# Where the values of a unit and the decay sums of the next stand among TensorE's products, and which queue issues the seam

## The chip, the cores and the metric

The kernel runs on one core of one Trainium2 chip. The metric is the device time of one execution in microseconds (us). Each execution is one launch, and the kernel before was run three times.

The engines are named as in the profile: PE is TensorE (matmul), PEld its weight load, DVE is VectorE, ACT is ScalarE, POOL is GpSimd, SP is SyncE. Each of them takes its instructions in the order of its own queue. POOL, ACT and SP also issue DMAs, and an issue stands in the queue like any other instruction.

## The reference

The first half is a gated recurrence over a sequence. For batch b (4), head h (8) and time t (768), with head size D = 48:

```python
mag = np.sqrt(a_re * a_re + a_im * a_im)
scale = np.minimum(mag, 0.999) / (mag + 1e-06)
a_re_n, a_im_n = (a_re * scale, a_im * scale)
for t in range(S):
    new_re = ar * S_re - ai * S_im      # ar, ai: a_re_n, a_im_n at time t
    new_im = ar * S_im + ai * S_re
    kv = np.einsum('bhd,bhe->bhde', k[:, :, t], v[:, :, t])
    S_re, S_im = (new_re + kv, new_im)
    y[:, :, t] = np.einsum('bhd,bhde->bhe', q[:, :, t], S_re)
```

The second half is a dense block on the result, laid out as 3072 tokens of 384 numbers: `h = x @ w_in` (384 by 2048), an ELU (`h` where it is positive, else `exp(h) - 1`), and `g @ w_out` (2048 by 384).

## The kernel before

**Units.** The work is cut into NU = 12 units. A unit is a chunk of C = 128 time steps of NB = 2 sequences, that is 256 tokens. Units 0 and 1 are the first chunks of the two pairs of sequences, units 2 and 3 the second chunks, and so on, so unit u + 2 carries on the state of unit u.

**The gates of a unit.** The recurrence is computed in chunks of L = 64 steps. The logarithm of the magnitudes and the angles of the gates are summed along time with matmuls, and q and k are scaled by the exponentials and turned by the sines and cosines of these sums. For a unit u > 1 the steps are: `squares` (ACT, L709 and L710), `joined` (the sum of the squares; POOL from unit 3 on, L716), `logarithms` (ACT, L735 and L736), `lengths` (DVE, L772), `powers` (ACT, L746 and L747), `ratios` (POOL, L759 and L760), `slopes` (DVE, L780), `angles` (ACT arctangent, L815), `carried` (DVE, L821, adds the angle of the chunk before to the first row), `turns` (PE sums at L832, DVE L837 and L840), `waves` (ACT sines, L967 to L971). `quartered` is the sum of the logarithms: four matmuls on PE (L883). `quarters_used` turns it into the factors E and F by six activations on ACT (L898), and writes the rows at the chunk's ends to a buffer in DRAM (L902), from where POOL fetches them as T (L951).

**The attention part of a unit.** `transposed` (PE L1013, ACT L1014) lays q and k with heads in the columns. From unit PAIRED = 4 on, `scored` is the first group of small products: the state products of both halves (L1054), then the scores of both (L1125), which DVE masks (L1133); the states are added on DVE (L1069) and scaled on POOL (L1071). `valued` is the second group: values times scores (L1087) and state times queries (L1096), both into the PSUM tile y; ACT copies y into the SBUF tiles x and y (L1156 and L1157). The heads do not fill x evenly, so `seam` moves six blocks of 16 partitions from y into x by DMA (L1169).

**The dense part of a unit.** `inner` multiplies x by w_in (L1189), `elu` applies the activation (ACT L1198 and L1199, DVE L1200). The second matmul is done by a scheme of seven products over four blocks: `folded` forms sums of blocks of g (DVE L1273), and `product(u, k, h)` does product k for half h, four matmuls each (L1295). They run in the order k = 1, 4 (half 0), 1, 4 (half 1), then 6, 5, 7, 2, 3, and gather in three PSUM banks. Product 1 is copied aside by ACT once its half 1 is done (L1303), and product 6 goes into the same bank and waits for that copy. DVE and ACT add up the rest (L1307, L1316, L1320, L1314), and SP sends the output (L1317). The matmuls are in fp32; the trace shows each as two pieces, so `x16` in it is eight matmuls of the program.

**The order.** Nothing is scheduled by a tool: the program writes the instructions in the order of a plan. The first part is a list by hand. For the rest, `put(at, fn, ...)` gives each step a due time, and the steps are written out by due time. A unit has SLOTS = 16 due times, and unit u starts at r = 16 (u - 2). Units overlap: while unit u is in its dense part, unit u + 1 is in its attention part and unit u + 2 in its gates. So due time r + 31 of unit u is r + 15 of unit u + 1.

In the kernel before, `valued` of units 4 to 10 stands at r + 31 and does three things: the values of both halves, then `quartered(u + 1)`, then the products with the state; after them it calls `quarters_used(u + 1, ...)`, and only then come the copies of y. `gates_of` therefore leaves out `decays` (which would call the same two functions) for units above PAIRED. The last unit, 11, has nobody after it, and its `valued` stands at r + 29.3. `seam` is issued from SP for the units from 4 on, from POOL for units 2 and 3.

Of the kernel before, what the change touches and what calls it, by code (L numbers as in the profile page):

```python
# [505 lines left out]
def kernel(  # L506
# [15 lines left out]
    NI, NF = DM // C, DF // C  # L522
# [3 lines left out]
    NU = B // NB * (S // C)  # L526
# [44 lines left out]
    def work(shape, tag="w"):  # L571
        return ps.tile(shape, FP32, tag=tag, bufs=3, name=tag)


    nat = [{} for _ in range(NU)]
# [110 lines left out]
    def flat(t):  # L686
        return t.rearrange("p n h d -> p (n h d)")
# [5 lines left out]
    def new(tag, bufs=1, shape=None):  # L693
        return sb.tile(shape or [C, NB, H, D], FP32, tag=tag, bufs=bufs, name=tag)
# [182 lines left out]
    def quartered(u):  # L877

        x = nat[u]
        both = [work([C, HD]) for n in range(NB)]  # L880
        for c in range(C // L):
            for n, t in enumerate(both):
                nc.tensor.matmul(  # L883
                    t[ts(c ^ n, L)], lhsT=sum_logs[ts(c, L), ts(c, L)],
                    rhs=flat(x["l"][ts(c, L), n : n + 1]), start=True, stop=True,
                )
        return both

    def quarters_used(u, both):

        x = nat[u]
        for n, t in enumerate(both):
            for key, sign in (("E", 1.0), ("F", -1.0)):
                pairs = [(slice(0, C), slice(0, C))]
                if n:
                    pairs = [(ts(c, L), ts(1 - c, L)) for c in range(C // L)]
                for to, of in pairs:
                    nc.scalar.activation(  # L898
                        out=flat(x[key][to, n : n + 1]), in_=t[of], func=AF.Exp, scale=sign
                    )  # L900
        ends = dram.tile([NB, C // L, H, D], FP32, tag="ends", bufs=2, name="ends")
        nc.scalar.dma_start(  # L902
            out=ends.rearrange("n c h d -> c n (h d)"),
            in_=x["E"][L - 1 :: L].rearrange("p n h d -> p n (h d)"),
        )
        x["ends"] = ends

    def decayed(u, n):
        x = nat[u]
        t = x["sums", n]  # L910
        for key, sign in (("E", 1.0), ("F", -1.0)):
            if u > 0 and n == 0:
                x[key] = new("n", 6)
            nc.scalar.activation(
                out=flat(x[key][:, n : n + 1]), in_=t, func=AF.Exp, scale=sign
            )

    def decays(u):
        x = nat[u]
        if u > 1:  # L920
            x["E"], x["F"] = new("n", 6), new("n", 6)
            quarters_used(u, quartered(u))
            return
        for n in range(NB):
            x["sums", n] = work([C, HD])
            nc.tensor.matmul(
                x["sums", n], lhsT=sum_logs, rhs=x["l"][:, n].rearrange("p h d -> p (h d)"),
                start=True, stop=True,
            )
            decayed(u, n)  # L930
# [68 lines left out]
    PAIRED = 4  # L999
# [83 lines left out]
    def value_products(u, n, y, first=True):  # L1083
        x = nat[u]
        for p, c, j in EACH:

            nc.tensor.matmul(  # L1087
                y[ts(j, HP), c, ts(p, L)], lhsT=vn[u % 2][ts(c, L), n, ds((2 * p + j) * D, HP)],
                rhs=x["a", n][ts(c, L), 2 * p + j], start=(first and p == 0), stop=False,
                skip_group_check=True,  # L1090
            )
    def carried_products(u, n, y):
        x = nat[u]
        for p, c, j in EACH:
            if x["S", n][c] is not None:
                nc.tensor.matmul(  # L1096
                    y[ds(j * HP, D), c, ts(p, L)], lhsT=x["S", n][c][:, 2 * p + j],
                    rhs=x["qt", n][:, 2 * p + j, ts(c, L)], start=False, stop=False,
                    skip_group_check=True,
                )  # L1100
# [37 lines left out]
    def valued(u):  # L1138

        x = nat[u]  # L1140
        y = ps.tile([C, C // L, 512], FP32, tag="y", bufs=1, name="y")
        for n in range(NB):
            value_products(u, n, y[:, :, ts(n, NP * L)], n == 0)
        if u + 1 < NU:
            both = quartered(u + 1)
        for n in range(NB):
            carried_products(u, n, y[:, :, ts(n, NP * L)])
        if u + 1 < NU:
            z = nat[u + 1]
            z["E"], z["F"] = new("n", 6), new("n", 6)  # L1150
            quarters_used(u + 1, both)
        x["x"], x["y"] = new("x", 2, [C, NI, GT]), new("y", 1, [C, GT])
        parts = y.rearrange("p c (n x t) -> p c n x t", n=NB, x=NP)
        to = x["x"].rearrange("p x (n c t) -> p c n x t", n=NB, c=C // L)
        for c in range(C // L):
            nc.scalar.copy(out=to[:, c], in_=parts[:, c, :, 0:NI])  # L1156
        nc.scalar.copy(  # L1157
            out=x["y"].rearrange("p (n c t) -> p c n t", n=NB, c=C // L), in_=parts[:, :, :, NI],
        )

    def seam(u):

        x = nat[u]
        for j in range(2):
            for i in range(NI):
                eng = nc.scalar if u < 2 and j else nc.gpsimd
                if u >= PAIRED or u == 0 and i == NI - 1:
                    eng = nc.sync
                eng.dma_start(  # L1169
                    out=x["x"][ds(j * HP + D, G), i], in_=x["y"][ds(j * HP + i * G, G)]  # L1170
                )
# [232 lines left out]
    def put(at, fn, *args):  # L1404
        if fn is hidden:
            plan.append((at, len(plan), inner, args))
            plan.append((at, len(plan), elu, args))
        else:
            plan.append((at, len(plan), fn, args))

    def decays_of(u, *at):
        fns = squares, logarithms, powers, lengths, ratios, slopes, noted, angles, carried
        put(at[0], begun, u)
        for x, fn in zip(at, fns):
            put(x, fn, u)
            if fn is squares:
                put(x, joined, u)

    def gates_of(u, *at):
        for x, fn in zip(at, (decays, turns, waves, scaled, ends, gated)):  # L1420
            if fn is not decays or u <= PAIRED:
                put(x, fn, u)

    def values_of(u, *at):
        fns = (transposed, "q"), (transposed, "k"), (scores,), (states,), (values,)
        for n in range(NB):
            for x, (fn, *key) in zip(at[5 * n :], fns):
                put(x, fn, u, *key, n)
        put(at[-1], seam, u)
# [64 lines left out]
    def layer_of(u, at_h, at_p):  # L1494
        for m in range(NF // 2):
            put(at_h[m], hidden, u, 2 * m)
        put(at_h[3], folded, u, 0)
        put(at_h[7], folded, u, 1)
        ks = [(1, 0), (4, 0), (1, 1), (4, 1)] + [(k, h) for k in (6, 5, 7, 2, 3) for h in range(2)]
        for m, (k, h) in enumerate(ks):  # L1500
            put(at_p[0] + m * len(at_p) / len(ks), product, u, k, h)

    for u in range(2, NU):
        r = (u - 2) * SLOTS
        put(r + 8, load_a, u)
        put(r + 8, load_v, u)
        put(r + 8, load_qk, u)
        if u == 2:
            decays_of(u, 16, 17, 17, 18.4, 19.5, 19.6, 22.7, 19.8, 19.8)
            gates_of(u, 20.4, 21.6, 22.1, 22.4, 22.4, 22.6)  # L1510
        else:
            decays_of(u, r + 11, r + 12, r + 12, r + 13.4, r + 13.5, r + 14.9, r + 16.7, r + 15.5, r + 16.6)
            gates_of(u, r + 15, r + 18, r + 18.5, r + 18, r + 18, r + 19.5)
        if u < PAIRED:
            values_of(u, *(max(r + 22, 24.5) + x for x in (0, 1, 2, 3, 5, 4, 5, 6, 7, 8, 9)))
        else:
            for n in range(NB):
                put(r + 22 + 2 * n, transposed, u, "q", n)
                put(r + 23 + 2.3 * n, transposed, u, "k", n)
            put(r + 26.6, scored, u)  # L1520
            put(r + (31 if u + 1 < NU else 29.3), valued, u)
            put(r + (31 if u + 1 < NU else 29.3), seam, u)
        layer_of(u, range(r + 36, r + 44), range(r + 44, r + 52))
    for m in range(NR):
        put(40 + 4 * m, test_fetch, m)
# [42 lines left out]
```

## Time and profile before

| | |
|---|---|
| three runs | 730.99, 731.03, 733.4 us; median 731.03 |
| the profiled execution | 733.4 us, span 731.7 us from first to last instruction |
| PE busy | 677.1 us, 93% of the span, 6656 instructions |
| PEld busy | 593.2 us, 81% |
| ACT busy | 398.5 us, 54% |
| DVE busy | 395.9 us, 54% |
| POOL busy | 176.0 us, 24% |
| mean granted clock of PE | 0.966 of full speed |
| HBM | 48.88 MB read, 4.78 MB written, 73 GB/s over the span |

How to read the lines that follow. A line of the timeline gives the start and the length in us, the engine, the line of the program, the operation, output and inputs by the program's names, partitions and shape, and how many such instructions in a row. Brackets at its end give the idle time ahead of it and who ended it. A length covers the time from the first start to the last end, and matmuls overlap a little, so from one group's start to the next group's start is the better measure of what a group takes. A line of the table of stages gives the window, its length, the busy time of PE, PEld, DVE, ACT and POOL with instruction counts, then the granted clock of PE, the share of the DMA engines and GB/s. A line of the view of waits names the waiting instruction, the one that released it, the total in us, how often, and the longest.

In this kernel the steady part, units 4 to 10, repeats with a period of 57.7 to 59.4 us; the seven stretches look alike, and the one from 430 to 462 us stands for them below.

### The profile page before, as it was taken

The page shows a single profiled execution, that of the slowest core. Times are in us where ns is not written, and L with a number is a line of the kernel's source. Part 1 is how long each engine was busy: PE and PEld are TensorE (multiplying, and loading weights), DVE is VectorE, ACT ScalarE, POOL GpSimd, SP SyncE. Part 2 cuts the span into 40 slices and gives each one's busy share as a digit, 9 for nine tenths or more (in the row PEclk, how much of TensorE's full clock was granted, in tenths as well). Part 3 has the DMA queues.
Part 4 walks back from the last instruction along what each step waited for, and adds up shares of the span by engine and source line. Part 5 has one row for each costly group of instructions (what it writes and reads, how often), then busy time and mean ns, then how long its engine had stood idle before and what let it go on. Part 6 is the DMA issues. An engine that isn't in the chain of part 4 may idle for free.

```text
span 731.7 us, 15769 instructions
## 1 busy us (share of the span) xinstructions
PE 677.1 (93%) x6656; PEld 593.2 (81%) x6656; DVE 395.9 (54%) x579; ACT 398.5 (54%) x622; POOL 176.0 (24%) x159
## 2 busy tenths in 40 slices
PE   8798899988999979979979998997997997999996
PEld 6787775665889879879879887997987986989995
DVE  5789999516666545454454553553644545433141
ACT  6765446578466456645653754655546654661230
POOL 2000000237145133151331431422413403310000
PEclk9889999999999989989999999998999999999999
DMA  9986555232536403701901901920730550200000
GB/s 166 168 144 110 141 172 130 51 61 50 77 77 110 93 23 88 115 22 49 154 23 40 142 23 33 152 41 25 125 77 22 116 86 24 72 1 7 22 1 27
DMA packets 149899, 55.98 MB, mean 77 GB/s; under 512 B 129172, under 2 KB 142652, under 8 KB 149820
## 3 DMA queue, kind: packets, MB, share of 16 engines
q1 hardware_dynamic: 147776, 54.32, 39.1%
q0 software_dynamic: 1824, 0.44, 0.8%
q8 instruction: 54, 0.88, 0.5%
q14 instruction: 25, 0.20, 0.1%
q10 hardware_dynamic: 220, 0.14, 0.1%
HBM read 48.88 MB, written 4.78 MB: 73 GB/s over the span
## 4 chain that ended last, share of the span: by engine, by line
PE 73%; issue 6%; ACT 5%; DVE 5%; POOL 5%; SPq 3%; DMA 2%; ACTq 0%; POOLq 0%; DVEq 0%
PE mlp L1189 28%; PE mlp L1295 22%; PE w L1013 5%; PE mlp L1210 4%; PE y L1096 3%; PE w L1054 2%; POOL n L716 2%; SPq L596 2%; PE y L1125 2%; PE y L1087 2%; PE w L832 2%; POOL S L1071 1%; PE w L1210 1%; ACT n L746 1%; ACT n L736 1%
## 5 line engine op out<-in xcount | busy, mean ns | idle before, releaser
L1189 PE MATMUL mlp<-x,w_in 128*128 128x256 f32 x1152 | 260.6, 381 | 2.6 <-DVE g L1200 2.6
L1189 PEld LDWEIGHTS mlp<-x,w_in 128*128 128x128 f32 x1152 | 214.6, 190 | 31.9 <-DVE g L1200 3.0
L1198 ACT ACTIVATE ee<-mlp 128x512 f32<-128x512 f32 x96 | 57.3, 597 | 144.1 <-PE mlp L1189 135.8
L1200 DVE SCALAR_TENSOR_TENSOR g<-ee,mlp 128x512 f32<-128x512 f32 x96 | 65.5, 685 | 126.2 <-ACT ee L1199 116.6
L1295 PE MATMUL mlp<-w_out,g 128*128 128x192 f32 x640 | 110.3, 326 | 0.0
L1295 PEld LDWEIGHTS mlp<-w_out,g 128*128 128x128 f32 x640 | 105.4, 190 | 2.7
L1295 PE MATMUL mlp<-w,g 128*128 128x192 f32 x320 | 70.5, 384 | 28.4 <-ACT ee L1303 28.4
L1295 PEld LDWEIGHTS mlp<-w,g 128*128 128x128 f32 x320 | 64.3, 227 | 31.9 <-ACT ee L1303 30.5
L1071 POOL TENSOR_TENSOR S<-S,T 128x384 f32<-128x384 f32 x36 | 29.3, 830 | 168.4 <-DVE S L1069 168.4
L1273 DVE TENSOR_TENSOR g<-g 128x512 f32<-128x512 f32 x80 | 67.2, 841 | 2.7
L1199 ACT ACTIVATE ee<-ee 128x512 f32<-128x512 f32 x96 | 60.5, 631 | 2.9
L898 ACT ACTIVATE n<-w 64x384 f32<-64x384 f32 (+1 forms) x60 | 28.1, 486 | 49.3 <-PE w L883 48.6
L856 POOL DMA_DIRECT2D carry<-n x10 | 5.3, 530 | 172.9 <-DVE n L840 172.9
L993 POOL TENSOR_TENSOR kg<-k,cs 128x1536 f32<-128x1536 f32 x9 | 41.0, 4551 | 20.1 <-issue 20.0
L1314 ACT COPY o<-mlp 128x192 f32<-128x192 f32 x10 | 3.2, 319 | 67.1 <-DMA out_dram<-o 56.3
L821 DVE SCALAR_TENSOR_TENSOR n<-carry,n 1x768 f32<-1x768 f32 x10 | 9.5, 946 | 45.3 <-ACT n L815 45.3
L1210 PE MATMUL mlp<-w_out,g 128*128 128x384 f32 x96 | 32.8, 490 | 0.7 <-DVE g L1200 0.7
L1014 ACT COPY qt<-w 128x512 f32<-128x512 f32 x48 | 25.6, 581 | 12.5 <-PE w L1013 12.5
L1295 PE MATMUL mlp<-wt,g 128*128 128x192 f32 x160 | 29.2, 327 | 0.0
L993 DVE TENSOR_TENSOR qg<-q,cs 128x1536 f32<-128x1536 f32 (+1 forms) x12 | 19.5, 1623 | 17.4 <-ACT cs L971 17.4
L716 POOL TENSOR_TENSOR n<-n 128x768 f32<-128x768 f32 x9 | 19.8, 2196 | 35.4 <-ACT n L710 35.4
L1013 PE MATMUL w<-ident,kg 128*128 128x128 f32 x192 | 26.0, 280 | 2.3 <-POOL kg L993 1.4
(173 smaller groups left out, 981.4 us busy)
## 6 DMA issues: line engine op xcount, KB each, us to landing
w<-in_moe_w_out_dram SPq DMA_DIRECT2D x8, 768.0 KB, 4.9
g<-in_moe_w_in_dram SPq DMA_DIRECT2D x16, 384.0 KB, 3.2
g<-in_moe_w_out_dram SPq DMA_DIRECT2D x16, 384.0 KB, 3.4
w<-in_moe_w_in_dram SPq DMA_DIRECT2D x16, 288.0 KB, 5.9
vn<-in_v_dram SPq DMA_DIRECT2D x24, 192.0 KB, 4.0
out_dram<-o SPq DMA_DIRECT2D x48, 96.0 KB, 2.1
ar<-in_a_re_dram SPq DMA_DIRECT2D x22, 192.0 KB, 4.6
ai<-in_a_im_dram SPq DMA_DIRECT2D x22, 192.0 KB, 7.5
```

The source lines that it names most:

```text
L716: products(u).tensor_tensor(out=x["m2"], in0=x["m2"], in1=x["sq"], op=ALU.add)
L898: nc.scalar.activation(out=flat(x[key][to, n : n + 1]), in_=t[of], func=AF.Exp, scale=sign)
L993: eng.tensor_tensor(out=to[:, :, :, 0:D], in0=each.unsqueeze(2).to_broadcast([C, step * H, 2, D]), in1=x["cs"][:, n * H : (n + step) * H], ...
L1013: nc.tensor.transpose(t[:, h], of, ident)
L1071: eng.tensor_tensor(out=new_s, in0=new_s, in1=wide, op=ALU.mult)
L1189: nc.tensor.matmul(t[:, e], lhsT=w_in[:, i, ts(f + e, C)], rhs=x["x"][:, i], start=(i == 0), stop=(i == NI - 1),)
L1198: nc.scalar.activation(out=e, in_=t, func=AF.Relu, scale=-1.0)
L1199: nc.scalar.activation(out=e, in_=e, func=AF.Exp, scale=-1.0)
L1200: nc.vector.scalar_tensor_tensor(out=x["g", f // 8][:, f % 8 : f % 8 + 2], in0=e, scalar=-1.0, in1=t, op0=ALU.add, op1=ALU.max)
L1210: nc.tensor.matmul(x["o", n], lhsT=x["g", f // 8][:, f % 8, ts(n, C)], rhs=w_out[:, f], start=(f == 0), stop=(f == NF - 1),)
L1273: nc.vector.tensor_tensor(out=S_of(u, k, h), in0=a, in1=b, op=op)
L1295: nc.tensor.matmul(to, lhsT=a[:, m], rhs=b[:, m], start=(first and h == 0 and m == 0), stop=False, skip_group_check=True,)
```

## The change

- `quartered` and `quarters_used` become one function again, `quartered`, which does the four sums, the six activations and the DMA of the ends. It is called by `decays`.
- `decays` is put for every unit, at its own due time r + 15. That is the place in the queues of PE and ACT where the four sums stood before; what is new is that they stand there alone.
- `valued` and `seam` stand at r + 29.3 for every unit, so for units 4 to 10 they move ahead by 1.7 due times. The products of L1295 that lie between are passed by `valued` on PE: k = 4 half 1 and both halves of k = 6. On ACT the copies of y now stand behind L1303 and ahead of the six activations of the next unit.
- `seam` of units 4 to 11 is issued by POOL. In POOL's queue the six DMAs of unit u (4 to 10) stand behind L716 and ahead of L759 and L760 of unit u + 1. They leave SP's queue, where they stood between two fetches of weights.

The order of the first group of small products is not touched, and the order of DVE's instructions is the same in both programs.

```diff
--- before.py
+++ after.py
@@ -884,11 +884,6 @@
                     t[ts(c ^ n, L)], lhsT=sum_logs[ts(c, L), ts(c, L)],
                     rhs=flat(x["l"][ts(c, L), n : n + 1]), start=True, stop=True,
                 )
-        return both
-
-    def quarters_used(u, both):
-
-        x = nat[u]
         for n, t in enumerate(both):
             for key, sign in (("E", 1.0), ("F", -1.0)):
                 pairs = [(slice(0, C), slice(0, C))]
@@ -919,7 +914,7 @@
         x = nat[u]
         if u > 1:
             x["E"], x["F"] = new("n", 6), new("n", 6)
-            quarters_used(u, quartered(u))
+            quartered(u)
             return
         for n in range(NB):
             x["sums", n] = work([C, HD])
@@ -1141,14 +1136,8 @@
         y = ps.tile([C, C // L, 512], FP32, tag="y", bufs=1, name="y")
         for n in range(NB):
             value_products(u, n, y[:, :, ts(n, NP * L)], n == 0)
-        if u + 1 < NU:
-            both = quartered(u + 1)
         for n in range(NB):
             carried_products(u, n, y[:, :, ts(n, NP * L)])
-        if u + 1 < NU:
-            z = nat[u + 1]
-            z["E"], z["F"] = new("n", 6), new("n", 6)
-            quarters_used(u + 1, both)
         x["x"], x["y"] = new("x", 2, [C, NI, GT]), new("y", 1, [C, GT])
         parts = y.rearrange("p c (n x t) -> p c n x t", n=NB, x=NP)
         to = x["x"].rearrange("p x (n c t) -> p c n x t", n=NB, c=C // L)
@@ -1164,7 +1153,7 @@
         for j in range(2):
             for i in range(NI):
                 eng = nc.scalar if u < 2 and j else nc.gpsimd
-                if u >= PAIRED or u == 0 and i == NI - 1:
+                if u == 0 and i == NI - 1:
                     eng = nc.sync
                 eng.dma_start(
                     out=x["x"][ds(j * HP + D, G), i], in_=x["y"][ds(j * HP + i * G, G)]
@@ -1418,8 +1407,7 @@
 
     def gates_of(u, *at):
         for x, fn in zip(at, (decays, turns, waves, scaled, ends, gated)):
-            if fn is not decays or u <= PAIRED:
-                put(x, fn, u)
+            put(x, fn, u)
 
     def values_of(u, *at):
         fns = (transposed, "q"), (transposed, "k"), (scores,), (states,), (values,)
@@ -1518,8 +1506,8 @@
                 put(r + 22 + 2 * n, transposed, u, "q", n)
                 put(r + 23 + 2.3 * n, transposed, u, "k", n)
             put(r + 26.6, scored, u)
-            put(r + (31 if u + 1 < NU else 29.3), valued, u)
-            put(r + (31 if u + 1 < NU else 29.3), seam, u)
+            put(r + 29.3, valued, u)
+            put(r + 29.3, seam, u)
         layer_of(u, range(r + 36, r + 44), range(r + 44, r + 52))
     for m in range(NR):
         put(40 + 4 * m, test_fetch, m)
```

## The prediction

> **What bounds the kernel now.** I read the page's busy table first: PE is busy for 677.1 us of a span of 731.7 us (93%), no other engine above 54%. So only two things can move the time much: PE standing still, and PE running slowly. The view of waits on PE shows where it stands still (columns: total us, times, longest).
>
> ```profile
> engine line waited for: us in total, times, longest us
> PE mlp L1295 <- ACT ee L1303: 28.4, 7, 4.1
> PE mlp L1189 <- DVE g L1200: 2.6, 1, 2.6
> ```
>
> One wait makes up most of it: seven times, once in each of units 4 to 10, PE stands before a product of L1295 until ACT has made the copy L1303. Next, PE's timeline through one such unit (start us, length us, what).
>
> ```profile
> 434.74 1.46 PE L1295 MATMUL mlp<-w_out,g 128*128 128x192 f32 x8
> 436.04 1.46 PE L1295 MATMUL mlp<-wt,g 128*128 128x192 f32 x8
> 441.56 4.35 PE L1295 MATMUL mlp<-w,g 128*128 128x192 f32 x16 [4.06 <-ACT ee L1303]
> 445.84 1.30 PE L1087 MATMUL y<-a,vn 64*64 64x64 f32 x64
> 446.97 0.82 PE L883 MATMUL w<-n,sum_logs 64*64 64x384 f32 x8
> 447.72 1.99 PE L1096 MATMUL y<-qt,S 128*48 128x64 f32 x64
> 449.64 2.87 PE L1295 MATMUL mlp<-w,g 128*128 128x192 f32 x16
> 452.35 4.06 PE L1295 MATMUL mlp<-w_out,g 128*128 128x192 f32 x24
> 456.25 1.45 PE L832 MATMUL w<-n,sum_turns 128*128 128x384 f32 x4
> ```
>
> The stall ends at 441.56. The sixteen matmuls behind it take 4.28 us to the next start; the same sixteen with other weights take 2.71 us at 449.64. The table of stages says why (PEclk is the third number from the end): the granted clock is half after the stall.
>
> ```profile
> 266.00:271.30 5.30, 5.30 (x17) 4.86 (x17) 0.00 (x0) 0.00 (x0) 3.35 (x2) 0.50 0.05 13
> 449.60:457.00 7.40, 7.40 (x48) 7.09 (x44) 2.93 (x4) 4.34 (x8) 0.00 (x0) 1.00 0.08 17
> ```
>
> The chain of waits shows what holds L1303: on ACT it is queued behind the squares, logarithms and powers of the next unit (L709 to L747, with two table loads and a wait for POOL's L716). Nothing of that is touched by the change.
>
> **The change on PE.** The instruction counts of PE, DVE and ACT stay. In the built order, the values group (L1087 and L1096) moves ahead of twelve products of L1295: it now stands between the w_out products at 434.74 and the wt products at 436.04, so before the wait. The four sums of the next unit (L883) stay where they were, now alone between large products. Unit 11 already has this order in the trace:
>
> ```profile
> 666.51 1.46 PE L1295 MATMUL mlp<-w_out,g 128*128 128x192 f32 x8
> 667.90 1.16 PE L1087 MATMUL y<-a,vn 64*64 64x64 f32 x64
> 668.99 1.99 PE L1096 MATMUL y<-qt,S 128*48 128x64 f32 x64
> 670.91 1.57 PE L1295 MATMUL mlp<-wt,g 128*128 128x192 f32 x8
> ```
>
> From 666.51 to the next products, at 672.32, it takes 5.81 us. Set on 434.74, PE is at the wait at 440.55 instead of 437.34, and L1303 still releases it at 441.56: a stall of 1.0 us. The group's operands are there by 436: both masked scores (DVE L1133) end at 431.8, the last state (POOL L1071) at 432.5, 3.5 us earlier.
>
> From the stall's end to the start of L832, the trace has 16.03, 15.45, 14.75, 14.69, 15.46, 14.74 and 14.67 us in the seven units, 105.8 us in all. Three terms change, over seven units:
> - The values group leaves: about 1.08 + 1.92 = 3.00 us a unit, 21.0 us.
> - The sixteen slow matmuls: from the stall's end to L1087 they take 5.42, 5.19, 4.48, 4.28, 5.19, 4.48 and 4.23 us, 33.3 us in all. At 2.71 us each they would take 19.0: 14.3 us saved, if the clock stays up.
> - L883 alone costs 0.80 us at 126.87, plus 0.11 us to refill, against 0.75 inside the group: 1.1 us lost.
>
> So PE alone would need 2.71 + 0.91 + 2.71 + 3.90 = 10.23 us a unit: 34.2 us saved.
>
> Does the clock stay up? Where PE waited 1.12 us (before L883 at 215.41), 1.31 us (168.17) and 1.42 us (181.67), the granted clock over these stretches is 1.00; it is 0.50 only behind waits of 4 us. I take the full 14.3; the bounds are 0 and 14.3. The Trainium skill ("TensorE: Matmul & The Clock Gate", Part 1) speaks against counting this: it puts the ramp's penalty at under 1% of a typical span. The rows give 14.3 us, 2.0%; by the page this term would be at most 7.3 us and the time about 7 us higher.
>
> **The change on POOL.** The six DMAs of seam (L1169) leave SP, where they cost 3.68 us of issue off the path, and enter POOL's queue ahead of L759 and L760. Both engines' queues are in order, so this is an added wait: POOL stands at the first DMA until ACT's L1157 is done.
>
> ```profile
> 166.12 2.94 POOL L1169 DMA_DIRECT2D x<-y  x6
> ...
> 435.15 2.30 POOL L716 TENSOR_TENSOR n<-n 128x768 f32<-128x768 f32 x1 [2.67 <-ACT n L710]
> 441.39 1.85 POOL L759 TENSOR_TENSOR n<-ar,n 128x768 f32<-128x768 f32 x1 [3.93 <-ACT n L747]
> 443.31 1.80 POOL L760 TENSOR_TENSOR n<-ai,n 128x768 f32<-128x768 f32 x1
> ```
>
> L759 used to start at 441.39. Now, from L1303's end at 441.52: copies L1156 and L1157, 1.13 us; six issues, 2.94; L759 and L760, 3.72 from start to end; DVE L780, 0.95; ACT L815, 0.84; DVE L821, 0.95; and six handovers of some 0.04, 0.25 in all. That is 10.78 us, or 10.75 from the stall's end, and L832 needs it. PE is there after 10.23. **So L832 becomes the new wait, 0.52 us a unit, 3.6 us in all.** ACT's L898 is no rival to it: L883 ends about 445.2, L898's six pieces take 2.9 us, a table load 1.28: 449.4, before L780's end at 450.4.
>
> Against the six issues the Trainium skill has a rule ("SBUF — State Buffer", "SBUF: two separate sides"): a DMA issued from GpSimd starves while VectorE holds the shared port. In the trace DVE's L780 ran at 166.20, beside the six issues, and they still took 2.94 us. By the rule, the one DVE piece that falls there now (L1307, 0.36 us) would add 2.5 us over seven units.
>
> What is behind L832: DVE does L796 and L799 (1.73 us) after L821, so L837 to L840, then L1314, the sines and qg come about 1.2 us later against PE. Covers: PE needs qg at 469.21 and DVE made it at 465.58 (3.6 us); kg 472.67 against 468.91 (3.8 us); the bank that the first inner product takes is freed by L1314 at 459.93 against 461.44 (1.5 us). All hold, so I cost this at nothing; if the tightest cover were short by 0.5 us, 3.5 us come on top. The seam's data land about 2 us after issue, at 447.6, and are wanted after 457. SP gains time that nobody waits for. The loads for the next unit are issued from 462.9, and their first reader runs about 28 us later. Unit 11's seam moves queues too, with 13 us to spare.
>
> **The sum**: 21.0 + 14.3 - 1.1 - 3.6 = 30.6; from the unrounded spans, 105.8 - 7 x 10.75 = 30.5 us. The profiled execution took 733.4 us (span 731.7): 733.4 - 30.5 = **702.9 us**. The median of the three runs is 731.03, 2.4 lower; the half clock lasts for different lengths from unit to unit, so this may be the clock's luck, and as that would leave the path, I forecast from the profiled run.
>
> **Rivals.**
> 1. *The clock falls anyway.* The stall of 1.0 us and the new wait at L832 might leave PE idle enough. Then the 14.3 us stay, PE needs 12.27 us to L832 and hides POOL's chain: 19.9 us saved, 713.5 us. Against: clock 1.00 around the three waits above.
> 2. *The issues are dearer on POOL.* The dearest DMA issue on POOL in the trace is L951's, 0.95 us. Six of these cost 2.75 us more, all on L832's path: 7 x 2.75 = 19.3, 722.2 us. Against: L1169 itself took 0.48 to 0.54 us, 17 times.
> 3. *POOL's queue becomes the bound: slower.* If each seam DMA held POOL until the one before it had landed (1.9 us), six would take 11.4 us instead of 2.94, and L832 would start 19.2 us after the stall's end instead of 15.1: 7 x 4.1 = 29 us slower, 762 us. It decides once the six hold POOL for more than 2.94 + 4.36 = 7.3 us. Against: at 166.12 six went out in 2.94 us.
> 4. *The stall is not filled,* because the values group waits at its new place as long as PE did: near 733 us. Against: the 3.5 us of slack of its last operand.
>
> **How the numbers follow.** Forecast (697 to 709: from no wait at L832, 699.2, with 2 us for luck, to the added 2.5 and 3.5 us) 0.68; rival 1, 0.16; rival 2, 0.06; rival 3, 0.06; rival 4, 0.04. The range takes the forecast and rival 1, 697 to 716, 0.84. Faster by over 0.5% (about what a measurement of this kernel can tell from no change): 0.68 + 0.16 + 0.06 = 0.90; within it, rival 4, 0.04; slower, 0.06.
>
> **What would show it.** Right: the wait for L1303 falls from 4.06 to about 1.0 us; the granted clock stays 1.00 behind it, with sixteen matmuls in 2.7 us; a wait of PE on L832 for DVE L821 appears, 0.5 us; L759 starts about 4.3 us later than L747 allows. Wrong: half clock behind the stall (rival 1), six issues well over 2.94 us (2 and 3), PE waiting before L1087 or L1096 (4), or a wait for qg, kg or a bank in the inner stage.

## The result, and the profile after

The changed kernel took 708.53 us (median of four runs, 707.88 to 713.71), the kernel before 731.01 us beside it (four runs, 729.57 to 733.4). The ratio is 0.9705, with a 95% interval of 0.9652 to 0.9757: about 3% faster. The forecast was 702.9 us with a range of 697 to 716, so the time lies inside the range and 5.6 us above the forecast. The profiled execution took 708.33 us with a span of 706.6 us. PE is busy for 668.8 us (95%), POOL for 198.0 us (it was 176.0), and the mean granted clock is 0.986 (it was 0.966).

The lines of the program behind the change moved up in the listing: L1295 is now L1284, L1303 is L1292, L1087 and L1096 are L1082 and L1091, L898 is L893, L1156 and L1157 are L1145 and L1146, L1169 is L1158, L951 is L946, L981 is L976, L1307 is L1296. The lines up to L883 keep their numbers.

The view of waits of PE, after (columns: total us, times, longest):

```profile
PE w L832 <- DVE n L821: 6.5, 7, 2.1
PE mlp L1284 <- ACT ee L1292: 5.9, 7, 0.9
```

The wait of 28.4 us is down to 5.9 us, and the wait that the prediction announced stands at the head of the list, with a longest of 2.1 us that it did not announce. PE's timeline through the unit that answers to the one shown of before (start us, length us):

```profile
421.30 1.46 PE L1284 MATMUL mlp<-w_out,g 128*128 128x192 f32 x8
422.69 1.16 PE L1082 MATMUL y<-a,vn 64*64 64x64 f32 x64
423.78 1.99 PE L1091 MATMUL y<-qt,S 128*48 128x64 f32 x64
425.71 1.57 PE L1284 MATMUL mlp<-wt,g 128*128 128x192 f32 x8
428.13 2.87 PE L1284 MATMUL mlp<-w,g 128*128 128x192 f32 x16 [0.85 <-ACT ee L1292]
430.93 0.88 PE L883 MATMUL w<-n,sum_logs 64*64 64x384 f32 x8
431.73 2.87 PE L1284 MATMUL mlp<-w,g 128*128 128x192 f32 x16
434.44 4.06 PE L1284 MATMUL mlp<-w_out,g 128*128 128x192 f32 x24
438.95 1.56 PE L832 MATMUL w<-n,sum_turns 128*128 128x384 f32 x4 [0.46 <-DVE n L821]
```

The values group runs where PE used to stand still. The stall is 0.85 us, and the sixteen matmuls behind it take 2.80 us to the next start, where they took 4.28. The row of the table of stages for them has the full clock (1.00, third number from the end):

```profile
428.10:430.90 2.80, 2.77 (x16) 2.57 (x16) 0.03 (x1) 1.01 (x3) 1.50 (x4) 1.00 0.04 11
```

POOL's timeline in the same unit shows the six issues in their new place, and L759 right behind them:

```profile
429.40 2.92 POOL L1158 DMA_DIRECT2D x<-y  x6 [5.39 <-ACT y L1146]
432.34 1.83 POOL L759 TENSOR_TENSOR n<-ar,n 128x768 f32<-128x768 f32 x1
434.25 1.80 POOL L760 TENSOR_TENSOR n<-ai,n 128x768 f32<-128x768 f32 x1
```

From the stall's end to L832 it takes 10.85, 10.84, 10.84, 10.82 and 10.85 us in five units (the working gave 10.75), but 12.43 us in the last two, 10 and 11 counted by the unit whose gates they are. There L832 waits for 2.06 us instead of 0.46. That is where the missing microseconds begin.

### The profile page after: what moved, and what is told of

Read it like the earlier page. It is cut to its first block, busy times and chain, and to the rows that moved or that the text cites. A ratio compares the mean times of both kernels' runs of the same rounds, so it can differ in the third digit from the quotient of the medians.

```text
span 706.6 us, 15752 instructions
## 1 busy us (share of the span) xinstructions
PE 668.8 (95%) x6656; PEld 581.0 (82%) x6656; DVE 399.4 (57%) x579; ACT 396.2 (56%) x622; POOL 198.0 (28%) x207
## 4 chain that ended last, share of the span: by engine, by line
PE 61%; POOL 11%; DVE 8%; ACT 8%; issue 7%; SPq 3%; DMA 2%; ACTq 0%; POOLq 0%; DVEq 0%
PE mlp L1178 29%; PE mlp L1284 11%; PE w L1008 5%; PE mlp L1199 4%; POOL x L1158 3%; PE w L1049 2%; POOL n L716 2%; SPq L596 2%; POOL n L759 2%; POOL n L760 2%; PE y L1120 2%; PE w L832 2%; DVE n L780 2%; POOL S L1066 1%; ACT L746 1%
## 5 line engine op out<-in xcount | busy, mean ns | idle before, releaser
L1284 PE MATMUL mlp<-w_out,g 128*128 128x192 f32 x640 | 111.8, 329 | 0.0
L1284 PEld LDWEIGHTS mlp<-w_out,g 128*128 128x128 f32 x640 | 106.9, 192 | 2.9 <-issue 0.3
L1284 PEld LDWEIGHTS mlp<-w,g 128*128 128x128 f32 x320 | 51.6, 190 | 13.1 <-ACT ee L1292 8.0
L1284 PE MATMUL mlp<-w,g 128*128 128x192 f32 x320 | 56.8, 331 | 6.0 <-ACT ee L1292 5.9
L1158 POOL DMA_DIRECT2D x<-y x65 | 31.7, 495 | 87.8 <-ACT y L1146 48.8
L856 POOL DMA_DIRECT2D carry<-n x10 | 5.3, 526 | 136.2 <-DVE n L840 136.2
L1303 ACT COPY o<-mlp 128x192 f32<-128x192 f32 x10 | 3.2, 318 | 67.9 <-DMA out_dram<-o 32.7
L893 ACT ACTIVATE n<-w 64x384 f32<-64x384 f32 (+1 forms) x60 | 28.1, 486 | 21.2 <-PE w L883 20.5
L780 DVE SCALAR_TENSOR_TENSOR n<-n 128x768 f32<-128x768 f32 x11 | 13.7, 1246 | 42.3 <-POOL n L760 42.3
L1284 PE MATMUL mlp<-wt,g 128*128 128x192 f32 x160 | 29.9, 331 | 0.0
L716 POOL TENSOR_TENSOR n<-n 128x768 f32<-128x768 f32 x9 | 19.8, 2200 | 35.5 <-ACT n L710 35.5
```

Of the source, the lines that this page charges most:

```text
L716: products(u).tensor_tensor(out=x["m2"], in0=x["m2"], in1=x["sq"], op=ALU.add)
L1158: eng.dma_start(out=x["x"][ds(j * HP + D, G), i], in_=x["y"][ds(j * HP + i * G, G)])
L1284: nc.tensor.matmul(to, lhsT=a[:, m], rhs=b[:, m], start=(first and h == 0 and m == 0), stop=False, skip_group_check=True,)
```

## Experiments

Three questions were open. Where does the gain come from? The theory, called F in the expectations, is that of the prediction: the values group fills the stall, and the half clock behind the stall goes with it. Its rivals are Q, that moving the seam's issues from SP to POOL helps by itself, and S, that taking the four sums out of the values group helps by itself. What is the clock's own share? And why is L832 late in two units of seven? Theory P for that is told at its experiment.

**The seam back on SP (e1_seam_sp).** The changed kernel, with only the queue of the seam undone:

```diff
-                if u == 0 and i == NI - 1:
+                if u >= PAIRED or u == 0 and i == NI - 1:
                     eng = nc.sync
```

> The changed kernel with the seam of units 4 to 11 back on SP; everything else as changed. Theory F (the gain is the values group filling the stall before product 6, and the clock that stays up with it): the gain stays whole, and POOL's chain to L832 goes: the seven waits of PE on L832 for L821 (6.5 us in the changed kernel) and the half clock behind the last of them (1.6 us) vanish, DVE L780 is 0.96 us in all units, the run is near 700 us (698 to 702). Rival Q (the gain comes from the seam leaving SP's queue): the gain goes, near 731 us.

It took 699.79 us (695.2 to 701.11), a ratio of 0.9547 (0.9498 to 0.9595) to the kernel before at 731.24. In its PE timeline L832 comes without a wait:

```profile
426.60 2.87 PE L1284 MATMUL mlp<-w,g 128*128 128x192 f32 x16 [0.84 <-ACT ee L1292]
...
436.81 1.45 PE L832 MATMUL w<-n,sum_turns 128*128 128x384 f32 x4
```

From the stall's end to L832 are 10.21 us; the prediction gave 10.23 for PE alone, and 699.2 us for the time without the new wait. So by the medians the move to POOL's queue costs 8.7 us (708.53 - 699.79), and the rest of the change is worth more than the change as made.

**The move of the queue alone (e2_before_seam_pool).** The kernel before, with the seam's issues on POOL and nothing else:

```diff
-                if u >= PAIRED or u == 0 and i == NI - 1:
+                if u == 0 and i == NI - 1:
                     eng = nc.sync
```

> The kernel before with the seam of units 4 to 11 on POOL; there it stands behind L760, so it delays nothing on the path. Theory F: no change, 730 to 734 us, with the seven waits of 4.06 us on L1303. Rival Q: most of the gain, 710 us or less.

731.32 us, ratio 1.0002 (0.9982 to 1.0021), and PE's wait for L1303 is unchanged, 28.4 us in seven:

```profile
PE mlp L1295 <- ACT ee L1303: 28.4, 7, 4.1
```

Rival Q falls. It also shows why the same queue costs nothing here and 8.7 us in the changed kernel: here `seam` stands after the long stall and after L759 and L760, so nothing that PE needs soon is behind it.

**The sums alone, the values late (e3_sums_alone_values_late).** The changed kernel, with the seam on SP and the values group back at its old due time:

```diff
-            put(r + 29.3, valued, u)
-            put(r + 29.3, seam, u)
+            put(r + (31 if u + 1 < NU else 29.3), valued, u)
+            put(r + (31 if u + 1 < NU else 29.3), seam, u)
```

> The changed kernel with values and seam of units 4 to 10 back at their late due time and the seam on SP: the sums of the next unit stand alone, behind the values group, and that is all that is left of the change. Theory F: 1 us slower than before at most, 730 to 735 us, seven waits of 4.06 us. Rival S (the gain comes from the sums leaving the values group): 710 us or less.

730.32 us, ratio 0.9978 (0.995 to 1.0005); PE's wait for L1292 is again 28.4 us in seven:

```profile
PE mlp L1284 <- ACT ee L1292: 28.4, 7, 4.1
```

Rival S falls: splitting the function without moving the values group is worth nothing that these runs can tell.

**The values early, but with the sums still inside (e4_fused_early).** The kernel before, with only the due time changed:

```diff
-            put(r + (31 if u + 1 < NU else 29.3), valued, u)
-            put(r + (31 if u + 1 < NU else 29.3), seam, u)
+            put(r + (29.45 if u + 1 < NU else 29.3), valued, u)
+            put(r + (29.45 if u + 1 < NU else 29.3), seam, u)
```

> The kernel before with its fused group (values, sums of the next unit, state products) moved ahead of products 4 and 6, where the changed kernel has the values group. The sums wait for DVE's L772, which ends at the same time as L1303, so PE stands in the middle of the group instead of behind it. Theory F: seven waits of about 4.3 us, now of L883 on L772, half clock behind them, 728 to 736 us. A theory by which the early place of the values alone brings the gain: 715 us or less.

732.76 us, ratio 1.0025 (1.0002 to 1.0048). The stall is not gone, it has another name. PE's timeline:

```profile
431.84 1.16 PE L1087 MATMUL y<-a,vn 64*64 64x64 f32 x64
437.33 1.56 PE L883 MATMUL w<-n,sum_logs 64*64 64x384 f32 x8 [4.33 <-DVE n L772]
438.82 2.89 PE L1096 MATMUL y<-qt,S 128*48 128x64 f32 x64
```

The four sums stand in the middle of the group and need DVE's L772 of the next unit, which waits for ACT's L746, just ahead of L1303 in ACT's queue. So PE stands 4.33 us before L883, and half the group stays behind the wait. Of these two edits only both together, out with the sums and forward with the rest, give the gain: e3 and e4 each have one and win nothing.

**The clock alone (e5_before_fill).** The kernel before, with sixteen matmuls of the identity into an unread tile put ahead of product 6, in the stall. The useful work stays in its order:

```diff
+    def fill(n):
+
+        t = work([C, C])
+        for _ in range(n):
+            nc.tensor.matmul(t, lhsT=ident, rhs=ident, start=True, stop=True)
...
+            if u + 1 < NU:
+                put(r + 30, fill, 16)
...
-    items += [x[2:] for x in sorted(plan, key=lambda x: x[:2]) if x[2:] not in items]
+    items += [x[2:] for x in sorted(plan, key=lambda x: x[:2]) if x[2] is fill or x[2:] not in items]
```

The last pair of lines lets `fill` pass a test that drops steps which the list by hand already has.

> The kernel before with sixteen extra matmuls (identity by identity, result unused, some 3.5 us at full clock) ahead of product 6 in units 4 to 10: the stall is filled with work that nobody needs, and nothing else moves. It measures the clock's share alone. My size: the clock stays 1.00, the sixteen pieces of product 6 take 2.7 us instead of 4.2 to 5.4, 14.3 us saved, 717 to 720 us. By the page's bound on the ramp (under 1% of the span), 724 us or more; if filling did not hold the clock, 731 us.

718.45 us (717.69 to 718.94), ratio 0.9821 (0.9781 to 0.9861), against 731.97 for the kernel before on the same chip. PE's timeline:

```profile
428.33 3.73 PE L1405 MATMUL w<-ident 128*128 128x128 f32 x32
432.55 2.87 PE L1295 MATMUL mlp<-w,g 128*128 128x192 f32 x16 [0.48 <-ACT ee L1303]
```

PE does the same useful work and waits for the same copy. It is merely not idle until then, and the sixteen matmuls behind take 2.80 us to the next start. This is worth 731.97 - 718.45 = 13.5 us, which is the share of the clock; by the interval of the ratio it is 10 to 16 us, and the prediction had 14.3.

**Why L832 is late in two units (e6_carry_all).** POOL's timeline in unit 10 of the changed kernel, and DVE's:

```profile
542.25 1.81 POOL L760 TENSOR_TENSOR n<-ai,n 128x768 f32<-128x768 f32 x1
544.02 1.82 POOL L976 TENSOR_TENSOR k<-k,n 128x768 f32<-128x768 f32 x1
```

```profile
544.10 2.55 DVE L780 SCALAR_TENSOR_TENSOR n<-n 128x768 f32<-128x768 f32 x1 [4.64 <-POOL n L760]
```

DVE's L780 is on the path to L832, and it takes 2.55 us here; in the unit ahead it takes 0.96:

```profile
490.10 0.96 DVE L780 SCALAR_TENSOR_TENSOR n<-n 128x768 f32<-128x768 f32 x1 [4.65 <-POOL n L760]
```

POOL's L976, the scaling of k, started 0.08 us before it and ended at 545.84, and L780 ended 0.81 us after that. In the other units L976 is not there at that time. Ahead of it in POOL's queue stands the DMA that carries the last row to unit u + 2 (L856), and this waits until DVE's L840, about 8 us later. Units 10 and 11 have no unit u + 2, so they have no such DMA, and nothing holds L976 back. Theory P says that L976 beside L780 makes L780 long, and that the missing DMA lets it run there. The experiment gives these two units a DMA of the same kind, whose result nobody reads:

```diff
-        if nxt < NU:
+        if nxt < NU or u >= PAIRED:
             carry[nxt] = new("carry", 2, [1, NB * HD])
```

> The changed kernel in which units 10 and 11 also issue the small carry DMA (L856, its result unused): it waits for DVE's L840, so POOL's L976 stands behind it and no longer runs beside DVE's L780. Theory P (L780 took 2.55 us in these two units because POOL's L976 had started 0.08 us ahead of it and held what both need): L780 is 0.96 us in all units, the two waits of 2.06 us at L832 fall to 0.47, the half clock behind the last one goes, 703 to 705 us. Rival (L780 is longer there for another reason, such as transfers at that time): no change, 708 us.

703.67 us (702.36 to 706.93), ratio 0.9611 (0.957 to 0.9651). POOL's and DVE's timelines in unit 10:

```profile
555.10 0.54 POOL L856 DMA_DIRECT2D carry<-n  x1 [8.10 <-DVE n L840]
555.65 1.82 POOL L976 TENSOR_TENSOR k<-k,n 128x768 f32<-128x768 f32 x1
```

```profile
547.04 0.96 DVE L780 SCALAR_TENSOR_TENSOR n<-n 128x768 f32<-128x768 f32 x1 [4.64 <-POOL n L760]
```

L976 starts 8.6 us after the end of L760, L780 is 0.96 us, and PE's wait at L832 is 3.3 us in seven, none over 0.5 us. An added DMA made the program 4.9 us faster (708.53 - 703.67). Theory P holds: L780 is long where L976 runs beside it. And 703.67 us is within 1 us of the forecast: with L832 waiting for 0.5 us in every unit, as the working had it, the kernel takes what was predicted. That it comes so close is in part luck: the forecast took the 30.5 us from the profiled execution, 733.4 us; taken from the median of 731.03 they give 700.5.

**Other work in the stall (e7_seam_sp_5_first, e8_before_5_first).** If F holds, any ready work will do. Product 5 does not need the bank that product 1 holds, so it can stand ahead of product 6. This is one edit, made in the kernel of e1 (e7) and in the kernel before (e8):

```diff
-        ks = [(1, 0), (4, 0), (1, 1), (4, 1)] + [(k, h) for k in (6, 5, 7, 2, 3) for h in range(2)]
+        ks = [(1, 0), (4, 0), (1, 1), (4, 1)] + [(k, h) for k in (5, 6, 7, 2, 3) for h in range(2)]
```

> The changed kernel with the seam on SP, and with product 5, which needs nothing of L1303, ahead of product 6. Theory F: the rest of the stall (0.85 us in seven units) goes too, PE waits for nothing in the steady part, 691 to 696 us.

> The kernel before with product 5 ahead of product 6 and nothing else: the stall is filled with other work, values and sums stay fused and late, the seam on SP. Theory F (any ready work in the stall will do): PE waits about 0.4 us for L772 instead of 4.06 for L1303, the clock stays 1.00, 690 to 696 us. A theory by which the place of the values is what matters: 725 us or more.

e7 took 691.01 us (689.75 to 691.87), ratio 0.9438 (0.9399 to 0.9477), and no wait of PE over 0.2 us is left in units 4 to 10; the sixteen matmuls of product 5 stand where the wait was:

```profile
420.30 2.76 PE L1284 MATMUL mlp<-w,g 128*128 128x192 f32 x16
422.99 0.88 PE L883 MATMUL w<-n,sum_logs 64*64 64x384 f32 x8
423.80 2.87 PE L1284 MATMUL mlp<-w,g 128*128 128x192 f32 x16
```

e8 took 693.13 us (691.2 to 694.07), ratio 0.9466 (0.9424 to 0.9508): swapping two numbers in the kernel before wins 38.8 us where the change wins 22.5. PE's timeline in e8:

```profile
418.78 2.77 PE L1295 MATMUL mlp<-w,g 128*128 128x192 f32 x16
421.48 1.16 PE L1087 MATMUL y<-a,vn 64*64 64x64 f32 x64
423.05 0.88 PE L883 MATMUL w<-n,sum_logs 64*64 64x384 f32 x8 [0.41 <-DVE n L772]
423.86 1.99 PE L1096 MATMUL y<-qt,S 128*48 128x64 f32 x64
425.78 2.87 PE L1295 MATMUL mlp<-w,g 128*128 128x192 f32 x16
```

Product 6 has taken the due times of product 5, which lie behind the values group. So the old stall holds product 5 (2.70 us to the next start) and then the start of the fused group as well; e8 does not leave the group behind the wait for L1303. That it is the filling, and not the group's place, that keeps the clock up is shown by e5.

The terms add up. The stall of 28.4 us and the clock of 13.5 go, and seven waits of 0.41 us for L772 come: 28.4 + 13.5 - 2.9 = 39.0, measured 38.8. In e7 those waits do not come, but L883 alone costs 1.1 us: 28.4 + 13.5 - 1.1 = 40.8, measured 41.0 (731.97 - 691.01). e7 beats both kernels.

## Why the prediction was right, and where its size was off

- **The stall.** Predicted 1.0 us, measured 0.85. The values group never waits at its new place, so rival 4 is out.
- **The clock.** Predicted to stay up, worth 14.3 us. It stays at 1.00 behind all seven stalls of 0.85 us, and e5 measures 13.5 us for it alone. The Trainium skill ("TensorE: Matmul & The Clock Gate", Part 1) puts the ramp's penalty at under 1% of a typical span. That sentence stands in a passage on the warm-up of a kernel, and it is no bound for one that stalls again and again: measured by e5 the penalty is 1.8% of this one (13.5 of 731.97), because the kernel paid it seven times, once behind each stall. One reading behind the term was wrong: the clock is not at 0.50 "only behind waits of 4 us". In the kernel before it falls at 36.59 behind a wait of 1.91 us (PE's L1096 at 35.77), and that speaks for rival 1:

```profile
33.18:36.59 3.41, 1.50 (x54) 1.29 (x54) 2.16 (x4) 2.54 (x4) 0.00 (x0) 1.00 1.18 165
36.59:40.00 3.41, 3.41 (x40) 3.32 (x42) 1.39 (x3) 3.38 (x5) 0.00 (x0) 0.50 1.11 173
```

- **L883 alone**, -1.1 us: the group takes 0.80 us from start to start, as in the row that it was taken from.
- **The six issues on POOL.** 2.92 us against a predicted 2.94, in the unit shown; 2.92 to 2.95 in the seven. Rivals 2 and 3, dearer issues or a full POOL queue, are out. DVE's L1296 ran for 0.36 us at 431.10, beside them, and they were no longer for it: the 2.5 us that the prediction put into the top of its range did not come. No run shows this term. The prediction drew it from the rule of the Trainium skill ("SBUF — State Buffer", "SBUF: two separate sides") on DMAs issued from GpSimd, but the page gives that rule for a DVE instruction in a two-port mode, and nothing here shows that L1296 runs in one. So these rows say nothing against the rule.
- **The later covers.** None gave way, but the tightest is thinner than worked out. PE takes qg at 452.02 and DVE has made it at 450.96: 1.1 us, where 3.6 - 1.2 = 2.4 was expected. From the stall's end qg came only 1.2 us earlier than before (22.83 against 24.02), while PE's turn came 3.8 us earlier (23.89 against 27.65). The prediction had only moved DVE's own work behind L821.
- **The step that was mis-sized** is the last term of the sum: "So L832 becomes the new wait, 0.52 us a unit, 3.6 us in all." In five units it is 0.46 to 0.48 us. In the last two it is 2.06, and the sum of all seven is 6.5.

What went wrong in that step: its chain took 0.95 us for DVE's L780 from the rows of before, without asking what POOL does beside it in each unit. In the kernel before, L976 (L981 there) waited in units 10 and 11 for ACT's L898, until 567.11 in the first of them, 5.7 us after L760. In the changed kernel L898 (now L893) no longer stands behind the values group and is earlier, and L760 is later by the six issues, so in unit 10 L893 is done at 542.72, ahead of L760 at 544.06, and L976 starts the moment L760 is done, which is the moment L780 starts too. It takes both: in e1, where the six issues are not on POOL, L976 of unit 10 still waits 3.11 us for L893, and L780 takes 0.96 us.

```profile
534.89 1.81 POOL L760 TENSOR_TENSOR n<-ai,n 128x768 f32<-128x768 f32 x1
539.81 1.82 POOL L976 TENSOR_TENSOR k<-k,n 128x768 f32<-128x768 f32 x1 [3.11 <-ACT n L893]
```

The prediction weighed a delay between DVE and POOL at the six DMA issues, where the runs show none, and not at L780, which shows it.

The step also has a second effect, and it is rival 1 in one place of seven. Behind the last wait of 2.06 us the clock falls:

```profile
604.14 1.73 PE L832 MATMUL w<-n,sum_turns 128*128 128x384 f32 x4 [2.06 <-DVE n L821]
605.66 5.62 PE L1284 MATMUL mlp<-w_out,g 128*128 128x192 f32 x24
```

The next 24 matmuls take 5.62 us instead of the 4.06 that they take in the unit shown above.

The account of the miss, by spans: the working gives 731.7 - 30.5 = 701.2 us, and the span was 706.6, so 5.4 us are to be found. L832 starts 0.09 us later than worked out in five units (0.4 us) and 1.68 us later in two (3.4 us). Behind its wait L832's own group takes 1.40 us to the next start against 1.29 without a wait (438.95 to 440.35 here, 436.81 to 438.10 in e1), which makes 0.8 us in seven. The half clock costs 1.6 us. That is 6.2 us. The 0.8 us of the other sign lie at the two ends: L832 of the unit ahead starts 0.17 us earlier than before (222.65 against 222.82), and what follows the last L832, without the terms above, is 0.7 us shorter. The experiments agree from the other side: e6, without the long waits and their half clock, is 4.9 us faster (2 x 1.59 + 1.6 = 4.8 by the rows), and e1, without any wait at L832, 8.7 us faster (6.5 + 0.8 + 1.6 = 8.9).

## What to carry to other kernels

A stall is filled by whatever is ready on that engine at that time; look for it in the whole plan, not only in the work that is being rearranged (e8, which swaps two products, won 38.8 us where the change won 22.5). Price a stall of PE by the slow stretch behind it as well as by its own length: here 13.5 us came on top of 28.4. And when a step's operands come earlier on one engine, list for every unit, the last ones too, what it will then run beside: a DMA that waits in a queue may have been keeping two instructions apart.

## What the runs showed of the hardware

**Two elementwise instructions beside each other.** POOL's L976 and DVE's L780 (both 128x768 in fp32) overlapped in two units. The one that started 0.08 us later took 2.55 us instead of 0.96, and it ended 0.81 us after the other, as if it had done nearly all its work only then. The Trainium skill ("SBUF — State Buffer", "SBUF: two separate sides") says that VectorE and GpSimd share a pair of ports as an exclusive lock, held for the whole instruction by whichever starts first, where the DVE instruction has two SBUF inputs and the GpSimd instruction reads SBUF, as both do here. The times agree with that. What e6 shows is that the delay goes when L976 is elsewhere; that the port is the reason is the page's word.

**Half clock after a partial idle.** Both waits of 2.06 us left PE idle for the same time, but only one had the half clock behind it. The table of stages, after, in windows of 3.4 us that end where the clock changed or could have: in each trace the half-clock stretches start on a grid of 3.41 us (the first two fields are the window and its length, then PE's busy time; the clock is third from the end):

```profile
547.40:550.80 3.40, 2.24 (x10) 1.72 (x11) 3.21 (x6) 0.12 (x1) 0.31 (x1) 1.00 0.55 119
...
602.00:605.40 3.40, 1.34 (x5) 0.87 (x5) 2.95 (x5) 0.84 (x1) 1.30 (x2) 1.00 0.54 117
605.40:608.80 3.40, 3.40 (x11) 3.14 (x11) 3.19 (x8) 0.32 (x1) 0.00 (x0) 0.50 0.21 60
```

Where 1.34 of 3.40 us were busy, the next 3.4 us ran at half clock; where 2.24 were busy, they did not. Waits of 0.85 us never had it behind them, and the seven of 4.06 us in the kernel before always did, for one or two such stretches. The kernel before narrows this down, where one stall falls into two windows (the stall ends at 441.56; the last row is from the stall that ends at 615.61):

```profile
435.95:439.36 3.41, 1.56 (x10) 1.26 (x8) 3.20 (x3) 3.12 (x4) 1.50 (x1) 1.00 0.00 0
439.36:442.77 3.41, 1.21 (x7) 1.21 (x8) 0.96 (x1) 2.14 (x4) 1.38 (x1) 1.00 0.38 115
442.77:446.18 3.41, 3.41 (x23) 2.97 (x25) 0.16 (x1) 0.00 (x0) 2.27 (x2) 0.50 0.00 0
...
610.03:613.44 3.41, 1.52 (x10) 1.22 (x8) 3.17 (x3) 3.12 (x4) 1.46 (x1) 1.00 0.00 0
```

Behind 1.56 and 1.52 of 3.41 us busy the clock stayed up; behind 1.21 it fell. With the 1.34 from above, the limit in this steady part lies between 1.34 and 1.52 us. So a wait of 2 us can go either way, by how it falls against these windows. It is no rule for every kind of work: near the start of the changed kernel, in a window with thirty-two matmuls of 128x2 (L935), PE counts as busy for 3.13 us and the clock fell all the same, so PE's busy time alone does not decide it:

```profile
45.61:49.02 3.41, 3.13 (x42) 2.83 (x41) 2.71 (x6) 3.35 (x6) 0.00 (x0) 1.00 1.25 198
49.02:52.43 3.41, 3.41 (x9) 2.71 (x9) 3.34 (x6) 1.92 (x2) 0.00 (x0) 0.50 1.06 209
```
